# One fused attention and feed-forward kernel, its 2,679 steps put into another order

## The chip, the cores and the metric

The kernel runs on one core of one Trainium2 chip. The metric is the device time of one execution in microseconds (us), lower being better. A profiled execution also has a span, from its first to its last instruction.

## The reference

Four batches of eight heads, 768 positions, 64 values a head. Each query sees the first few keys ("sinks") and a window of up to 128 keys behind it. The result, laid out as 3072 tokens of 512 values, goes through a two-layer block with a SoLU (h times its softmax) and a layer norm between.

```python
scores = scale * np.matmul(q, k.transpose(0, 1, 3, 2))
keep = is_sink | in_window            # n_sink = 4, window = 128
a = softmax(np.where(keep, scores, -1e9)); x = np.matmul(a, v)
h = x @ w_in                          # 512 -> 1024
solu = h * softmax(h)
ln = (solu - mean(solu)) / np.sqrt(var(solu) + 1e-06) * g_ln
out = ln @ w_out                      # 1024 -> 512
```

## The kernel before, in words

The 3072 tokens are cut into 24 chunks of 128, numbered n = 0 to 23 (chunk 0 and 1 are the first chunks of two batches, then the rest follow batch by batch). A chunk goes through a long chain of steps, and the steps of some four to six chunks are under way at once:

- `turn_q`, `take_q`, `rest_q`, `swap_q`: the queries are transposed, split into a rounded high part and a rest (tile `qT`), and a copy with its halves exchanged (`qX`) is made by two DMA transfers of the SP queue.
- `take_k`, `rest_k`: the same split for the keys, into the tile `ring`.
- `score` (TensorE, 8 heads, two matmuls each, lines 656 and 657) writes into one of two PSUM banks, `bank_0` and `bank_1`. `pick` (line 663) and `mask` (line 674), both on VectorE, read the bank out; only then may another score use it.
- `exps`, `invert`, `normalise`: exponentials on ScalarE, sums inverted on VectorE, product on GpSimd. For chunks 8 to 22 that are not the first of their batch, `store_p` and `load_p` send the probabilities through DRAM (tiles `pn`, `pd`, `pb`) and `flip_p` finishes the transpose; others are transposed on TensorE (`turn_p`).
- `part_new`, `part_old` (GpSimd, lines 741 and 747) cut the transposed probabilities for two key chunks, and `value` (32 small matmuls, line 795) forms the attention output `av`.
- `x_hi`, `x_lo` (tiles `xh`, `xl`, lines 800 and 804), then `hidden` (8 steps of three matmuls, line 815), `highest`, `solu_exp`, `solu`, `centre`, `store_u`, `load_u`, `flip_u`, `u_hi`, `u_lo` (tiles `uh`, `ul`), and `project` (8 steps of three matmuls, line 902; 16 half ones in the last chunk), `scale` and `store`.

Ahead of and among the first chunks the weights are brought in: sixteen blocks are fetched (`wraw`), taken out of their 64-bit form by `lower_w` on ScalarE (line 421, tile `wps`) and `move_w`, `sign_w`, `rest_w` on VectorE (lines 425, 429, 435), and split in two parts (`w1h`, `w1l`, `w2h`, `w2l`).

What sets the order is one table. `ORDER` is a permutation of the numbers of all 2,679 steps; the kernel calls each step in turn, and each step's instructions and DMA issues go to the end of their engine's queue. Every engine works its own queue in order, so an instruction whose input isn't there holds up all that stands behind it on that engine. The pools hand out buffers in the same order.

```python
    for at in ORDER:
        f, n, i = steps[at]
        f(n, i)
```

The two score banks are handed out in the order in which they come free:

```python
    def claim(key, uses):
        held[key] = [banks.pop(0), uses]
        return held[key][0]
    def done(*key):
        held[key][1] -= 1
        if held[key][1] == 0:
            banks.append(held.pop(key)[0])
```

Of the kernel before, what the change touches and what calls it, by code (L numbers as in the profile page):

```python
# [19 lines left out]
    346, 0, 143, 2, 144, 244, 60, 348, 351, 5, 6, 3, 69, 350, 7, 51, 8, 352, 24, 9, 147, 154, 345, 12, 42, 155, 353,  # L20
    146, 156, 148, 10, 11, 61, 248, 255, 256, 257, 62, 63, 166, 15, 245, 167, 4, 182, 183, 64, 165, 160, 70, 181, 71,
    176, 66, 78, 33, 187, 72, 164, 157, 180, 158, 52, 145, 161, 186, 162, 177, 184, 163, 73, 449, 75, 178, 349, 53,
    259, 25, 54, 55, 179, 185, 26, 27, 189, 356, 87, 188, 74, 76, 77, 16, 361, 465, 28, 358, 17, 18, 191, 65, 67, 43,
    247, 360, 68, 249, 44, 45, 193, 354, 94, 19, 30, 29, 31, 57, 263, 266, 32, 136, 279, 267, 355, 34, 46, 282, 1,
    357, 359, 56, 58, 283, 268, 48, 35, 36, 453, 59, 37, 101, 79, 80, 21, 258, 47, 49, 460, 284, 81, 50, 761, 88, 82,
    190, 261, 39, 277, 262, 278, 89, 285, 90, 38, 40, 265, 264, 41, 115, 281, 280, 91, 95, 192, 194, 20, 22, 96, 362,
    97, 195, 108, 208, 286, 370, 23, 365, 246, 289, 98, 84, 291, 373, 209, 378, 381, 83, 85, 363, 210, 364, 122, 371,
    86, 293, 372, 102, 211, 379, 380, 103, 137, 138, 288, 212, 553, 213, 104, 287, 139, 116, 367, 290, 109, 215, 216,
    217, 450, 387, 375, 117, 292, 383, 110, 218, 140, 386, 461, 105, 214, 295, 294, 390, 219, 369, 462, 366, 129, 377,
    296, 374, 385, 220, 382, 118, 309, 310, 392, 402, 404, 368, 463, 221, 452, 311, 455, 454, 456, 451, 394, 396, 398,  # L30
    376, 316, 13, 317, 312, 119, 223, 92, 388, 384, 389, 347, 400, 313, 314, 458, 557, 457, 226, 93, 464, 459, 391,
    406, 554, 318, 222, 564, 111, 319, 141, 142, 130, 393, 403, 466, 395, 99, 472, 405, 474, 131, 407, 397, 555, 399,
    762, 315, 401, 224, 480, 482, 657, 408, 467, 475, 227, 488, 483, 490, 320, 470, 478, 321, 468, 409, 565, 476, 410,
    132, 486, 484, 556, 411, 471, 559, 558, 322, 412, 417, 479, 487, 492, 418, 561, 567, 473, 230, 560, 413, 123, 419,
    562, 481, 489, 493, 232, 469, 477, 566, 661, 495, 563, 414, 485, 100, 668, 415, 491, 659, 324, 124, 497, 125, 420,
    658, 494, 507, 499, 568, 576, 325, 765, 112, 865, 772, 584, 867, 126, 496, 416, 506, 508, 234, 509, 592, 501, 503,
    421, 498, 500, 572, 511, 580, 502, 504, 574, 235, 582, 588, 229, 505, 590, 422, 660, 512, 663, 423, 570, 662, 513,
    514, 578, 327, 670, 665, 667, 113, 586, 664, 666, 672, 515, 516, 228, 573, 581, 328, 425, 669, 571, 579, 133, 517,
    106, 589, 587, 594, 107, 225, 518, 519, 577, 675, 595, 671, 866, 585, 114, 521, 428, 120, 522, 523, 134, 593, 597,
    598, 868, 575, 121, 236, 237, 683, 583, 591, 596, 691, 524, 135, 676, 599, 231, 233, 600, 680, 127, 601, 426, 238,  # L40
    432, 610, 424, 429, 430, 684, 611, 692, 602, 604, 688, 612, 128, 674, 613, 520, 696, 431, 331, 682, 690, 615, 606,
    698, 764, 616, 677, 603, 605, 869, 685, 239, 525, 608, 693, 607, 333, 766, 240, 526, 241, 609, 768, 870, 242, 678,
    686, 329, 767, 330, 332, 527, 334, 617, 427, 699, 618, 769, 771, 335, 694, 702, 704, 336, 434, 770, 681, 773, 619,
    620, 679, 775, 621, 687, 433, 774, 695, 1083, 435, 776, 1092, 1091, 1094, 337, 338, 339, 436, 340, 780, 788, 700,
    341, 689, 697, 701, 706, 437, 622, 872, 1093, 703, 796, 778, 786, 871, 1189, 623, 529, 532, 781, 708, 705, 714,
    716, 794, 342, 789, 797, 873, 715, 717, 707, 803, 875, 536, 785, 709, 719, 323, 326, 779, 711, 625, 720, 787, 530,
    795, 1197, 874, 793, 624, 801, 243, 626, 784, 710, 792, 800, 627, 876, 343, 344, 878, 805, 534, 880, 783, 1199,
    782, 628, 790, 791, 713, 799, 887, 798, 1198, 884, 877, 535, 629, 883, 879, 881, 712, 1200, 630, 439, 802, 440,
    721, 885, 722, 1295, 631, 441, 723, 724, 633, 886, 806, 976, 804, 808, 818, 890, 898, 889, 977, 1082, 978, 906,
    729, 807, 725, 809, 726, 727, 980, 728, 810, 763, 634, 897, 528, 533, 905, 888, 636, 537, 1399, 730, 896, 442,  # L50
    812, 438, 820, 539, 904, 443, 932, 541, 891, 899, 1402, 907, 979, 913, 637, 981, 731, 732, 894, 982, 893, 814,
    1401, 638, 816, 819, 821, 901, 811, 813, 444, 733, 823, 815, 824, 734, 632, 445, 446, 902, 735, 447, 910, 817,
    639, 538, 825, 985, 987, 826, 909, 912, 916, 827, 543, 828, 640, 895, 540, 903, 911, 915, 918, 892, 900, 908, 448,
    1188, 829, 830, 991, 993, 1400, 914, 737, 983, 1001, 1009, 1095, 736, 833, 917, 928, 834, 919, 999, 1007, 831,
    1084, 641, 635, 929, 990, 931, 998, 542, 992, 835, 836, 1000, 1085, 1008, 921, 1006, 986, 1086, 920, 1015, 930,
    988, 923, 933, 832, 975, 934, 740, 1081, 1087, 996, 1014, 922, 1004, 531, 997, 837, 738, 1089, 925, 838, 927,
    1294, 924, 1005, 1013, 1012, 926, 1088, 1018, 544, 545, 935, 546, 547, 1017, 1020, 995, 839, 643, 994, 1403, 1002,
    1003, 1011, 1022, 936, 741, 937, 1010, 744, 548, 743, 642, 938, 549, 1016, 939, 1034, 1036, 840, 645, 1103, 1019,
    742, 841, 1100, 1511, 940, 1111, 1119, 1021, 1035, 1190, 1192, 1037, 1023, 844, 941, 942, 1099, 1194, 1025, 745,
    739, 644, 1026, 1108, 1303, 1116, 842, 550, 1305, 551, 1039, 646, 943, 1040, 1027, 944, 1107, 1115, 1304, 945,  # L60
    946, 1098, 1106, 1024, 647, 947, 1041, 1114, 1406, 746, 846, 747, 648, 1306, 1101, 1109, 1121, 1117, 649, 1122,
    650, 1029, 1028, 1030, 1032, 552, 948, 1096, 1097, 749, 748, 651, 652, 653, 1404, 654, 1104, 1112, 1105, 1113,
    1120, 1031, 1124, 1033, 1102, 1296, 1204, 1212, 1191, 655, 1042, 1043, 845, 751, 1298, 752, 1126, 847, 1128, 1140,
    1142, 848, 949, 951, 1044, 1110, 1118, 1045, 1123, 1202, 1193, 1300, 952, 1210, 1125, 1195, 1046, 1047, 843, 656,
    1220, 1205, 1218, 1048, 1127, 1129, 1213, 849, 750, 1141, 1143, 1049, 1221, 1050, 850, 950, 852, 1203, 1211, 1145,
    1208, 1146, 1051, 1297, 1052, 1216, 1224, 1219, 1053, 1209, 1227, 1217, 954, 1225, 1293, 854, 753, 754, 755, 756,
    851, 1226, 853, 1229, 1054, 1207, 1409, 1215, 1206, 1214, 1230, 1130, 1132, 855, 1232, 1133, 1131, 1223, 1222,
    1405, 1228, 757, 758, 856, 1234, 1310, 1187, 1055, 1135, 759, 1318, 1134, 1136, 1246, 1308, 957, 1138, 1299, 1301,
    1326, 857, 858, 859, 958, 1311, 1316, 1324, 955, 1057, 1147, 1058, 1248, 1231, 1137, 1309, 1417, 1408, 1139, 1410,
    1319, 1327, 1317, 1148, 956, 1325, 1332, 1412, 1233, 1235, 1510, 860, 1312, 1519, 1149, 1414, 1320, 1328, 1314,  # L70
    1322, 1419, 760, 1333, 861, 1330, 1336, 1521, 1150, 862, 1338, 1247, 1239, 1315, 1323, 1313, 1331, 1335, 1249,
    1237, 1321, 1418, 1151, 1329, 1155, 1152, 959, 1420, 960, 1411, 961, 1238, 1156, 1236, 1425, 1340, 1251, 963,
    1509, 1520, 1252, 1522, 1441, 1334, 1424, 1440, 1153, 1512, 1157, 1337, 1339, 1447, 1060, 1353, 1158, 1241, 1154,
    1243, 1341, 863, 1240, 1723, 1242, 962, 965, 966, 1355, 967, 1732, 1413, 1415, 1253, 1063, 1061, 1159, 1343, 1160,
    1244, 1245, 1254, 1344, 1617, 1625, 1523, 1345, 968, 964, 1064, 1629, 1734, 969, 1161, 1342, 864, 1255, 1162,
    1256, 1352, 1354, 1422, 1423, 1731, 1513, 1438, 1439, 1514, 1733, 970, 1428, 1444, 1446, 1429, 1445, 1257, 1515,
# [1044 lines left out]
```

## Time and profile before

| what | us |
|---|---|
| device time, median of three runs | 440.33 |
| the three runs | 438.46, 440.33, 1389.28 |
| span of the profiled execution | 437.9 |
| TensorE busy in it | 415.4 (95%) |
| VectorE busy | 360.9 (82%) |
| ScalarE busy | 315.7 (72%) |
| GpSimd busy | 234.2 (53%) |

The profile gives the span of its execution and no device time of its own beside it; the span lies 0.56 us under the fastest run and 2.43 us under the median. Busy time of TensorE is that of matmuls, whose ends are modelled and overlap; idle time is what no instruction covers. PEld stands for the weight loads of TensorE, which go beside the matmuls; a wait of a weight load that an earlier matmul outlasts costs less than it shows. DVE is VectorE, ACT ScalarE, POOL GpSimd, SPq the queue that issues the DMA transfers.

### The profile page before, as it was taken

What the parts mean: (1) busy time and instruction counts of PE and PEld (TensorE: products, weight loads), DVE (VectorE), ACT (ScalarE), POOL (GpSimd) and SP (SyncE); (2) the same over time, 40 slices, a digit from 0 to 9 for tenths busy, and PEclk for the clock granted to TensorE, in tenths of its full rate; (3) what the DMA queues carried; (4) which work ended last, traced back from release to release, by engine and by line L of the source; (5) the groups of instructions that cost most, each with busy time, mean ns of one, the idle gap of its engine ahead of it and who ended that gap; (6) DMA issues with size and microseconds to landing.
All of it is one profiled execution on the core that took longest, in us unless ns stands there. A gap on an engine that the chain in (4) does not pass through costs nothing.

```text
span 437.9 us, 8516 instructions
## 1 busy us (share of the span) xinstructions
PE 415.4 (95%) x2507; PEld 332.6 (76%) x2507; DVE 360.9 (82%) x1029; ACT 315.7 (72%) x817; POOL 234.2 (53%) x388
## 2 busy tenths in 40 slices
PE   4899999999999999999999999999999999999994
PEld 3447777878787888878777787878878778888884
DVE  2989999997999889999989997899899797674520
ACT  5989988978877776877768576768767675555551
POOL 7742626658867552788454736556623673624020
PEclk9999999999999999999999999999999999999999
DMA  8999449999899899976998989966966558623001
GB/s 225 324 284 293 96 101 168 180 151 196 218 161 216 208 185 253 195 229 190 180 239 210 207 219 226 193 173 179 269 176 216 170 165 227 188 96 121 24 26 55
DMA packets 164025, 81.38 MB, mean 186 GB/s; under 512 B 120188, under 2 KB 150788, under 8 KB 163972
## 3 DMA queue, kind: packets, MB, share of 16 engines
q1 hardware_dynamic: 163972, 80.77, 82.3%
q8 instruction: 22, 0.36, 0.4%
q14 instruction: 31, 0.25, 0.2%
HBM read 45.62 MB, written 23.72 MB: 158 GB/s over the span
## 4 chain that ended last, share of the span: by engine, by line
PE 53%; DVE 25%; DMA 6%; issue 5%; POOL 4%; ACT 4%; SPq 1%; DVEq 0%; POOLq 0%; ACTq 0%
PE o L902 18%; PE h L815 17%; PE av L795 5%; DVE qT L600 4%; DVE sc L674 3%; DVE bank L663 3%; PE bank L656 3%; PE bank L657 2%; PE ws L443 2%; DMA pb<-pd 2%; DVE ul L890 2%; DVE nm L820 2%; PE bank L654 2%; DMA wraw<-in_moe_w_in_dram 1%; DVE pt L725 1%
## 5 line engine op out<-in xcount | busy, mean ns | idle before, releaser
L685 ACT ACTIVATE sc<-sc,nmx 128x132 f32<-128x132 f32 (+1 forms) x192 | 75.9, 396 | 25.1 <-DVE nmx L674 24.1
L902 PE MATMUL o<-w2h,uh 128*128 128x512 f32 (+1 forms) x200 | 79.7, 398 | 0.0
L815 PE MATMUL h<-w1h,xh 128*128 128x512 f32 x192 | 77.0, 401 | 1.0 <-DVE u L830 0.9
L902 PE MATMUL o<-w2h,ul 128*128 128x512 f32 (+1 forms) x200 | 77.0, 385 | 0.5 <-DVE ul L890 0.5
L902 PE MATMUL o<-w2l,uh 128*128 128x512 f32 (+1 forms) x200 | 77.2, 386 | 0.0
L815 PE MATMUL h<-w1h,xl 128*128 128x512 f32 x192 | 75.9, 395 | 0.6 <-DVE xl L804 0.5
L815 PE MATMUL h<-w1l,xh 128*128 128x512 f32 x192 | 75.3, 392 | 0.0
L625 POOL TENSOR_TENSOR ring<-kf,ring 64x512 fp32r<-64x512 f32 x48 | 63.1, 1320 | 22.6 <-ACT ring L620 18.7
L674 DVE CUSTOM_DVE_ANT_0 sc<-bank,bias 128x132 f32<-128x132 f32 (+1 forms) x192 | 53.1, 288 | 9.4 <-PE bank L654 1.7
L704 POOL TENSOR_TENSOR pn<-sc,rs 128x512 f32<-128x512 f32 x26 | 28.0, 1079 | 53.1 <-DVE rs L691 19.2
L656 PE MATMUL bank<-ring,qT 128*128 128x264 f32 (+1 forms) x176 | 51.0, 300 | 1.9 <-DVE nmx L674 1.7
L657 PE MATMUL bank<-ring,qX 128*128 128x264 f32 (+1 forms) x176 | 48.3, 284 | 0.1
L700 POOL TENSOR_TENSOR sc<-sc,rs 128x528 f32<-128x528 f32 (+1 forms) x22 | 24.8, 1127 | 40.8 <-DVE rs L691 24.0
L902 PEld LDWEIGHTS o<-w2h,ul 128*128 128x128 f32 x200 | 37.5, 188 | 9.2 <-DVE ul L890 1.2
L902 PEld LDWEIGHTS o<-w2h,uh 128*128 128x128 f32 x200 | 37.6, 188 | 8.8 <-issue 3.1
L741 POOL TENSOR_SCALAR_AFFINE_SELECT pc<-pt 128x512 f32<-128x512 f32 x40 | 28.4, 716 | 29.4 <-DVE pt L725 25.5
L815 PEld LDWEIGHTS h<-w1h,xl 128*128 128x128 f32 x192 | 36.0, 188 | 10.6 <-DVE xl L804 2.8
L656 PEld LDWEIGHTS bank<-ring,qT 128*128 128x128 f32 x176 | 33.1, 188 | 12.0 <-DVE nmx L674 6.3
L815 PEld LDWEIGHTS h<-w1h,xh 128*128 128x128 f32 x192 | 36.1, 188 | 7.3 <-issue 0.8
L902 PEld LDWEIGHTS o<-w2l,uh 128*128 128x128 f32 x200 | 37.7, 188 | 5.0
L825 ACT ACTIVATE e<-h,nm 128x1024 f32<-128x1024 f32 x24 | 26.7, 1113 | 18.7 <-DVE nm L820 18.6
L815 PEld LDWEIGHTS h<-w1l,xh 128*128 128x128 f32 x192 | 36.2, 188 | 5.0
(146 smaller groups left out, 975.9 us busy)
## 6 DMA issues: line engine op xcount, KB each, us to landing
qX<-qT SPq DMA_DIRECT2D x88, 128.0 KB, 2.7
ud<-u SPq DMA_DIRECT2D x20, 512.0 KB, 4.3
ub<-ud SPq DMA_DIRECT2D x80, 128.0 KB, 3.5
pd<-pn SPq DMA_DIRECT2D x26, 256.0 KB, 3.0
pb<-pd SPq DMA_DIRECT2D x52, 128.0 KB, 3.4
vn<-in_v_dram SPq DMA_DIRECT2D x24, 256.0 KB, 4.3
out_dram<-ob SPq DMA_DIRECT2D x23, 256.0 KB, 2.6
kn<-in_k_dram SPq DMA_DIRECT2D x12, 384.0 KB, 6.6
```

The lines of the kernel that those rows point to most:

```text
L625: nc.gpsimd.tensor_tensor(t[ROWS[1 - x]], src[ROWS[x]], t[ROWS[x]].bitcast(F32), op=ALU.subtract)
L656: nc.tensor.matmul(o, st["qT", n, x][:, r, :], rhs, start=True, stop=False)
L657: nc.tensor.matmul(o, st["qX", n, x][:, r, :], rhs, start=False, stop=True)
L674: nc.vector.tensor_tensor_reduce(out=st["sc", n, hb][:, j, c0:c1], in0=st["s", n, h].rearrange("p a x -> p (a x)")[:, c0:c1], in1=bias0 if ...
L685: nc.scalar.activation(sc[:, i, c0:c1], sc[:, i, c0:c1], AF.Exp, bias=nmx[:, i:i + 1], scale=-1.0, accum_out=ssum[:, i:i + 1])
L700: nc.gpsimd.tensor_tensor(sc[:, :, c0:c1], sc[:, :, c0:c1], rs.unsqueeze(2).to_broadcast([P, HB, c1 - c0]), op=ALU.mult)
L704: nc.gpsimd.tensor_tensor(pn.rearrange("p g h f -> p h g f"), sc[:, :, 4:SEG].rearrange("p h (g f) -> p h g f", f=32), rs.unsqueeze(2).uns ...
L741: nc.gpsimd.affine_select(pc, st["pt", n, hb], pattern=[[0, HB], [1, P]], compare_op=ALU.is_ge, fill=0.0, base=0, channel_multiplier=-1)
L795: nc.tensor.matmul(acc[ROWS[x], r, :], vals[:, 2 * r + x, :], p[:, 2 * jp + x, :], start=alone, stop=alone or (r, i) == (NPAIR - 1, 1))
L815: nc.tensor.matmul(st["h", n][:, cols], a[:, kt, :], w[:, kt, cols], start=(kt == 0 and m == 0), stop=(kt == KT1 - 1 and m == 2))
L825: nc.scalar.activation(e, st["h", n], AF.Exp, bias=st["nm", n], scale=1.0, accum_out=se)
L902: nc.tensor.matmul(st["o", n, i], a[:, kt % 4, :], part(w, kt)[:, i * wide:(i + 1) * wide], start=(kt == 0 and m == 0), stop=(kt == KT2 - ...
```

## The change

The table `ORDER` is another permutation of the same 2,679 numbers; nothing else in the file differs. Each engine therefore has the same instructions, in another sequence. Two of its lines, the first before and the first after:

```diff
 ORDER = (
-    346, 0, 143, 2, 144, 244, 60, 348, 351, 5, 6, 3, 69, 350, 7, 51, 8, 352, 24, 9, 147, 154, 345, 12, 42, 155, 353,
+    143, 147, 154, 2070, 882, 1437, 3, 253, 196, 269, 1302, 2476, 203, 1431, 168, 298, 2098, 2099, 569, 301, 2102,
 )
```

In front of each name in the rows below stands the line of the code; the number in a tile's name behind the chunk (`kf_1`, `qX_16_0`) tells the chunk, the last one only the place in the program's list of tiles, which differs between the two programs.

**ScalarE at the start of the program**, before. `kf_0` and `kf_1` are the transposed keys of chunks 0 and 1 on their way out of their PSUM bank, `wps_5` is the first weight block:

```order
L615 COPY kf_0_171<-bank_1_90 128x512
L620 CAST ring_127<-kf_0_171 64x4x128 x2
L588 COPY qf_0_194<-bank_1_90 128x512
L421 ACTIVATE wps_5_211<-wraw_5_138 128x512
L615 COPY kf_1_217<-bank_0_89 128x512
L620 CAST ring_127<-kf_1_217 64x4x128 x2
```

And now:

```order
L615 COPY kf_0_135<-bank_0_89 128x512
L261 CAST ident_r_96<-ident_91 128x128
L620 CAST ring_127<-kf_0_135 64x4x128
L592 CAST qT_2_0_145<-bank_1_90 64x512
L308 COPY val_58<-spread_0_158 128x2
L592 CAST qT_2_1_188<-bank_1_90 64x512
L588 COPY qf_0_201<-bank_0_89 128x512
L310 COPY g_sb_99<-spread_1_156 128x8
L615 COPY kf_1_204<-bank_1_90 128x512
L421 ACTIVATE wps_5_206<-wraw_5_176 128x512
L620 CAST ring_127<-kf_0_135 64x4x128
```

The copy of `kf_1`, which frees the second score bank, stood behind the first weight block's lowering and now stands ahead of it.

**TensorE between the last value matmul of chunk 17 and its first hidden matmul**, before. `o_14` is the second layer's output of chunk 14, the banks take scores of chunk 19:

```order
L795 MATMUL av_17_4180<-pt_17_1_4118,vn_16_3877 64x128 x2
L902 MATMUL o_14_0_4102<-w2h_3_716,uh_14_1_4082 128x512
L902 MATMUL o_14_0_4102<-w2l_3_717,uh_14_1_4082 128x512
L902 MATMUL o_14_0_4102<-w2h_3_716,ul_14_1_4084 128x512
L656 MATMUL bank_1_90<-ring_127,qT_19_0_3951 128x264
L657 MATMUL bank_1_90<-ring_127,qX_19_0_4091 128x264
L656 MATMUL bank_0_89<-ring_127,qT_19_0_3951 128x264
L657 MATMUL bank_0_89<-ring_127,qX_19_0_4091 128x264
L815 MATMUL h_17_4241<-w1h_62,xh_17_4213 128x512
```

And now the same stretch's first rows:

```order
L795 MATMUL av_17_4129<-pt_17_1_4146,vn_16_3874 64x128 x2
L902 MATMUL o_14_0_4137<-w2h_2_745,uh_14_1_4168 128x512
L902 MATMUL o_14_0_4137<-w2l_2_746,uh_14_1_4168 128x512
L902 MATMUL o_14_0_4137<-w2h_2_745,ul_14_1_4170 128x512
L732 MATMUL ptp_18_0_4226<-ident_91,sc_18_0_3982 128x128 x4
L656 MATMUL bank_1_90<-ring_127,qT_19_0_3980 128x264
L657 MATMUL bank_1_90<-ring_127,qX_19_0_4064 128x264
L656 MATMUL bank_0_89<-ring_127,qT_19_0_3980 128x264
L657 MATMUL bank_0_89<-ring_127,qX_19_0_4064 128x264
L902 MATMUL o_14_0_4137<-w2h_2_745,uh_14_1_4168 128x512
```

One project step and two scores stood between the two; now it is four project steps (the second begins in the last row), three scores and a group of transposes.

**The SP queue at the exchange of chunk 16's queries**, before. `pn_15` is written to `pd_15` when GpSimd has normalised chunk 15; `out` is a result:

```order
L913 DMA out_0_dram<-ob_9_0_3312 128x512
L609 DMA qX_16_0_3407<-qT_16_0_3290 64x512
L610 DMA qX_16_0_3407<-qT_16_0_3290 64x512
L609 DMA qX_16_1_3425<-qT_16_1_3370 64x512
L610 DMA qX_16_1_3425<-qT_16_1_3370 64x512
L714 DMA pd_15_3449<-pn_15_0_3374 512x1x128
L862 DMA ud_12_3451<-u_12_3377 128x1024
```

And now:

```order
L714 DMA pd_15_3441<-pn_15_0_3379 512x1x128
L609 DMA qX_16_0_3443<-qT_16_0_3294 64x512
L610 DMA qX_16_0_3443<-qT_16_0_3294 64x512
L862 DMA ud_12_3460<-u_12_3317 128x1024
L536 DMA vn_15_3462<-in_v_dram 128x8x64
L714 DMA pd_15_3441<-pn_15_1_3438 512x1x128
L609 DMA qX_16_1_3558<-qT_16_1_3364 64x512
L610 DMA qX_16_1_3558<-qT_16_1_3364 64x512
```

Both exchanges of chunk 16 stood ahead of the writes of chunk 15's probabilities; each now stands directly behind one.

## Rows read from the trace of the kernel before

**Rows 1.** The page: the span, and the busy time of each engine (share of the span) with its number of instructions.

```profile
span 437.9 us, 8516 instructions
PE 415.4 (95%) x2507; PEld 332.6 (76%) x2507; DVE 360.9 (82%) x1029; ACT 315.7 (72%) x817; POOL 234.2 (53%) x388
```

**Rows 2.** Busy time by stretches of the span; behind each engine's time its number of instructions, then the granted clock, the share of the DMA engines and GB/s.

```profile
0.00:11.00 11.00, 5.38 (x21) 4.21 (x21) 2.37 (x9) 5.92 (x12) 7.72 (x31) 1.00 0.82 225
11.00:66.00 55.00, 50.69 (x270) 35.63 (x271) 52.09 (x159) 50.99 (x134) 25.51 (x34) 1.00 0.78 219
66.00:198.00 132.00, 128.65 (x824) 104.49 (x822) 120.56 (x348) 104.93 (x278) 85.94 (x128) 1.00 1.07 197
198.00:330.00 132.00, 128.96 (x782) 104.42 (x779) 119.12 (x340) 93.46 (x251) 74.40 (x122) 1.00 0.94 204
330.00:414.00 84.00, 83.44 (x509) 68.10 (x509) 61.99 (x170) 53.20 (x134) 37.99 (x67) 1.00 0.53 155
414.00:438.00 24.00, 18.31 (x108) 15.78 (x107) 4.78 (x7) 7.24 (x12) 2.70 (x8) 0.99 0.11 37
```

**Rows 3.** The waits of TensorE's weight loads from 66 to 414 us: waiting operation and line, what it waited for, us in total, times, longest.

```profile
PEld bank L656 <- DVE nmx L674: 4.8, 10, 1.2
PEld av L795 <- POOL pt L747: 3.6, 8, 0.8
...
PEld h L815 <- DVE xl L804: 2.3, 6, 0.9
...
PEld bank L657 <- DMA qX<-qT: 0.4, 1, 0.4
```

**Rows 4.** The start in order of time, TensorE, ScalarE and VectorE: start, duration, engine, line, operation, tiles, and in brackets the idle time before it with what ended it.

```profile
11.54 0.79 PE L654 MATMUL bank<-kf,qf 64*128 64x128 f32 x2 [1.50 <-ACT kf L615]
...
10.35 0.62 ACT L421 ACTIVATE wps<-wraw 128x512 f32<-128x512 f32 x1 [1.16 <-DMA wraw<-in_moe_w_in_dram]
10.91 0.58 ACT L615 COPY kf<-bank 128x512 f32<-128x512 f32 x1
...
11.01 0.70 DVE L425 TENSOR_SCALAR wps<-wps 128x512 int32<-128x512 int32 x1 [3.00 <-ACT wps L421]
12.35 0.28 DVE L674 CUSTOM_DVE_ANT_0 sc<-bank,bias 128x128 f32<-128x128 f32 x1
12.77 0.68 DVE L435 SCALAR_TENSOR_TENSOR wbits<-wraw,wps 128x512 int32<-128x512 int32 x1
```

**Rows 5.** Groups of instructions by line with shapes kept apart: count, busy us, mean ns of one, idle time before them.

```profile
L800 ACT CAST xh<-av 128x512 fp32r<-128x512 f32 x24 | 13.9, 581 | 8.6 <-PE av L795 8.4
L804 DVE TENSOR_TENSOR xl<-av,xh 128x512 fp32r<-128x512 f32 x24 | 16.3, 681 | 1.6 <-ACT xh L800 1.4
L663 DVE COPY_PREDICATED bank<-m_cur,bank 128x128 f32<-128x128 int32 x88 | 24.2, 285 | 7.7 <-PE bank L657 7.2
L674 DVE CUSTOM_DVE_ANT_0 sc<-bank,bias 128x132 f32<-128x132 f32 x160 | 44.7, 289 | 6.2 <-POOL sk L763 0.8 <-PE bank L657 0.2
L674 DVE DVE_READ_ACCUMULATOR2_ANT nmx<- 128x1 f32 x192 | 15.8, 82 | 0.0
L656 PE MATMUL bank<-ring,qT 128*128 128x264 f32 x160 | 47.2, 305 | 1.9 <-DVE nmx L674 1.7
```

**Rows 6.** Pieces of the chain of work that ended last: start, time in the chain, engine, tile, line, number of instructions.

```profile
246.39 1.90 PE av L795 x32
250.58 0.13 PE bank L656
250.71 0.12 PE bank L657
252.47 0.69 PE h L815 x3
```

**Rows 7.** What the SP queue waited for in front of its issues (us, times, longest), and the issues of the query exchange with the median us from issue to landing.

```profile
SPq L714 <- POOL sc L708: 20.3, 11, 3.7
SPq L720 <- DMA pd<-pn: 13.6, 8, 3.1
SPq L867 <- DMA ud<-u: 13.5, 6, 3.7
...
qX<-qT SPq DMA_DIRECT2D x88, 128.0 KB, 2.7
```

**Rows 8.** VectorE's two split operations with both inputs in SBUF and with one in PSUM (`bank`, `utp`), and the spread of the second over single instructions (shortest/median/longest ns).

```profile
L600 DVE TENSOR_TENSOR qT<-qf,qT 64x512 fp32r<-64x512 f32 x34 | 30.5, 898 | 2.3 <-ACT qT L592 1.3
L600 DVE TENSOR_TENSOR qT<-bank,qT 64x512 fp32r<-64x512 f32 x10 | 6.9, 689 | 2.2 <-ACT qT L592 1.9
L890 DVE TENSOR_TENSOR ul<-ur,uh 128x512 fp32r<-128x512 f32 x40 | 30.6, 772 | 3.1 <-ACT uh L886 2.9
L890 DVE TENSOR_TENSOR ul<-utp,uh 128x512 fp32r<-128x512 f32 x8 | 5.5, 686 | 10.7 <-ACT uh L886 10.6
L890 DVE TENSOR_TENSOR ul<-ur,uh x40: 651/686/1445, 101.7 to 413.6; 128x512 fp32r<-128x512 f32 x40
```

**Rows 9.** The tail: the maximum of the last chunk's hidden layer, its scaled copy on ScalarE, and the last piece of the chain.

```profile
414.49 1.23 DVE L820 TENSOR_REDUCE nm<-h 128x1 f32<-128x1024 f32 x1 [0.25 <-PE h L815]
418.31 1.15 ACT L843 ACTIVATE ud<-u,nmu 128x1024 f32<-128x1024 f32 x1 [1.30 <-DVE u L830]
...
424.57 7.75 PE o L902 x57
```

262 rows, old and new, of the table ORDER are left out of this document.

## The prediction, made before the changed kernel was run

> **What bounds the kernel now.** I read the page first: TensorE is busy 415.4 of 437.9 us [rows 1], so an order can only fight over the 22.5 us in which it has nothing to do, and over waits that hide inside its busy time. The table by stretches says where those lie [rows 2]. The first 11 us hold 5.6 us of idle TensorE. From 11 to 66 us three engines are nearly full (VectorE 52.1, ScalarE 51.0, TensorE 50.7 of 55 us): the weights are taken apart there, and VectorE has the least room. From 66 to 414 us TensorE runs 341.05 of 348 us, idle 3.35 + 3.04 + 0.56 = 6.95 us in the three rows together. The last stretch has 5.7 us of idle, nearly all after the last matmul. TensorE's granted clock is 0.99 to 1.00 in every one of these rows, that is 2.4 GHz, the idle first stretch included; I expect no term from it.
>
> The waits of TensorE's weight loads name who is late in the long middle [rows 3]: the mask that empties a score bank (4.8 us in ten waits), GpSimd's cut of the probabilities (3.6 us in eight), the rest of the attention output, `xl` (2.3 us in six). A query exchange was late once, by 0.4 us. These are the only things that another order can better there, and the first it can worsen.
>
> **The change part by part.** Every engine keeps its instructions, so no busy time goes or comes by itself. A whole table has moved, and I can't sum 2,679 moves one by one; I take the four places where rows show TensorE waiting, count in both orders how often the cause stands, and price each case from its row.
>
> *Start.* TensorE's second score waits 1.50 us for the copy of `kf_1`, since that copy (10.91 us) stands on ScalarE behind a weight block's lowering, which itself waits 1.16 us for its fetch [rows 4]. Now the copy stands ahead, so the 1.5 us go, with the 0.62 us of the lowering at most: 2.1 us for TensorE. But the stretch behind it is VectorE's. VectorE gains only what it can do in its own 3.00 us of idle time before 11.01 us: two masks, which took the 0.42 us from 12.35 to 12.77 [rows 4]. Bounds: 2.1 us gained; nothing, if the first weight block comes later than now. I take -0.4 us, the value of the engine that is full from 11 to 66 us.
>
> *Value to hidden.* The first hidden matmul of a chunk needs `xh` and `xl`, 0.58 + 0.68 = 1.26 us after the last value matmul [rows 5]. Measuring TensorE's work between them with 0.69 us for a hidden or project step and 0.25 us for a score [rows 6], 7 of the 24 chunks have less than 1.26 us before and 4 now (chunk 17 goes from one project step and two scores, 1.2 us, to 3.9 us). A case costs 2.3 us / 6 = 0.38 us [rows 3]; three fewer give -1.15 us. Bounds: 0, if what is behind `xl` is late anyway, and -2.3 us for all six.
>
> *Score banks.* A score needs the mask of the score that held its bank. I count a pair as short when TensorE's work between the two is less than VectorE's queue from that pick to that mask (0.29 us a pick, 0.29 + 0.08 us a mask, and what is put between) plus 0.30 us for the first score's own matmul [rows 5]. From chunk 3 on there are 10 short pairs before and 15 now, and what they lack adds up to 3.1 us before and 4.7 us now. I take +1.6 us. Priced by the wait's mean, 4.8 us / 10 [rows 3], the five more would be +2.4 us, the upper bound; the lower bound is 0, where VectorE runs ahead of TensorE.
>
> *The SP queue.* It waits 13.6 us for `pd` and 13.5 us for `ud` to be written before it may read them back [rows 7]. Between a chunk's last write of `pd` and the first read stand 31 other steps on SP in the 13 chunks together, 25 before; for `ud` 85 in 20 chunks, 64 before. The queue will stand still less; no large wait of TensorE names these transfers [rows 3], so I give this 0, at best -1 us. Against it, of the query exchanges that stand directly behind a write of `pd` there are 8 now and 4 before, chunk 16's two among the new ones. Such a write waits for GpSimd, 20.3 us in 11 waits [rows 7]. Directly behind a write of `ud` or a result there are 3 now and 8 before, which is why I give the whole 0. This cover, that exchanges come early, is worth the most if it is gone; that is the second rival.
>
> *Tail.* After the last hidden matmul, maximum, exponential, product and scaled copy run from 414.49 to 418.31 + 1.15 = 419.46 us, 5.0 us, and TensorE has other projects to do meanwhile; the chain ends with matmuls [rows 9]. Between that matmul and the first transpose of the last chunk there are now ten project steps, 6.9 us, where there were twelve. Still cover: 0. If it were gone, it would cost what is lacking of the 5.0 us.
>
> Sum: -0.4 - 1.15 + 1.6 + 0 + 0 = about 0, a span of 438.0 us against 437.9. The device times shown stand 0.56 and 2.43 us above the span (438.46 and the median of 440.33); with 1.5 us, midway, I forecast **439.5 us**.
>
> *A rule on shared ports.* VectorE's split takes 898 ns with both inputs in SBUF and 689 ns with one in PSUM, the other split 772 against 686 ns, and one and the same form ranges from 651 to 1445 ns [rows 8]. Something outside these instructions lengthens them, by 34 x 209 + 40 x 86 ns = 10.5 us in all. The Trainium skill, "SBUF — State Buffer", section "Who interferes with whom", says that a VectorE instruction with two SBUF inputs contends with a GpSimd instruction that reads SBUF, and that whichever comes first keeps the other out. These rows agree with it; by that rule the 10.5 us depend on which of them happen to meet, so on the order.
>
> **The rivals.** *Faster by over 2%.* All 6.95 us of idle between 66 and 414 us go, and 2.1 us at the start with them: 439.5 - 9.05 = 430.5 us. For it speaks that the DMA read-backs have more room; against it that this takes nearly every wait of the middle, while the count of short bank pairs goes up, and that the first 66 us belong to VectorE, not to TensorE.
>
> *Slower by over 2%: the query exchange comes late.* An exchange needs 2.7 us from issue to landing and now stands four times more behind a write that waits for GpSimd, a mean of 20.3 / 11 = 1.85 us and at most 3.7 us [rows 7]. If each such wait reaches TensorE, it costs 7.4 to 14.8 us; taking the middle, 439.5 + 11 = 450.5 us. It decides once the wait exceeds the lead that the exchange has over its first score. Against it: that wait was 0.4 us in the whole middle [rows 3], and fewer exchanges now stand behind results.
>
> *More meetings on the ports.* If twice as many of the two-input splits are lengthened, VectorE has 10.5 us more to do [rows 8]. It is idle 11.4 us of 132 in the first of the middle's stretches and more later [rows 2], so about half would reach TensorE: 439.5 + 5.3 = 444.8 us, 1% slower. The opposite, all lengthening gone, gives 434.3 us.
>
> *The change does less than the table suggests.* Both orders keep each chunk's steps within a few us of the same place in TensorE's work, and the waits just land elsewhere; that is my forecast in other words, and gives the same time.
>
> **How the numbers follow.** Two per cent of 440.33 is 8.8 us, about what a measurement of this kernel can tell from no change. The forecast, within 2% with waits that move but add up to the same, gets 0.72; ports that meet more or less often 0.05, also within 2%. The faster rival gets 0.10: it needs every gain at once. The slower one gets 0.13: a new order of this size has more ways to lose a lead than to find one in an engine that is 95% busy, but its counts are mixed. So faster 0.10, same 0.77, slower 0.13. The range of 432 to 450 us covers the forecast, both port cases (434.3 and 444.8) and the slower rival up to its middle, and leaves out the faster one and the rest of the slower one, about 0.16.
>
> **What would show it.** In the changed profile: TensorE busy close to 415 us, and 5 to 9 us idle between 66 and 414 us; the 1.50 us wait for `kf_1` gone, with VectorE's first weight step still near 11 us; weight loads waiting for `xl` under 2.3 us and for the bank's mask over 4.8 us; the tail's last piece again one run of matmuls. I am wrong if a weight load waits for `qX` by several us (the exchange), if VectorE's busy time leaves 361 us by over 5 us (the ports), or if a long wait stands in the tail.

## The result, and the profile after

The changed kernel takes 428.29 us (median of four runs, 427.67 to 429.0), the kernel before 441.46 us beside it (438.46 to 1389.28, four runs); the ratio is 0.9735, with a 95% interval of 0.9692 to 0.9778. It is 2.65% faster, below the range that I gave. The run of 1389.28 us stands far off all the others and is left out of the ratio. The profiled execution took 428.25 us, 1.75 us more than its span.

The page of the changed kernel: span and busy times, to be read against [rows 1].

```profile
span 426.5 us, 8500 instructions
PE 410.2 (96%) x2507; PEld 333.3 (78%) x2507; DVE 347.4 (81%) x1029; ACT 313.4 (73%) x817; POOL 231.9 (54%) x388
```

The span is 11.4 us shorter. VectorE does the same 1,029 instructions in 13.5 us less, and TensorE's busy time fell by 5.2 us, which, with equal instructions at an equal clock, speaks for waits that had been hidden inside it (the ends of matmuls are modelled).

The same stretches as in [rows 2], changed kernel.

```profile
0.00:11.00 11.00, 5.45 (x21) 4.00 (x21) 2.36 (x9) 4.91 (x11) 7.25 (x30) 1.00 0.84 214
11.00:66.00 55.00, 51.23 (x273) 35.94 (x272) 50.43 (x156) 52.15 (x135) 25.04 (x35) 1.00 0.81 226
66.00:198.00 132.00, 131.47 (x852) 109.11 (x852) 120.12 (x364) 108.58 (x289) 88.55 (x134) 1.00 1.05 202
198.00:330.00 132.00, 132.00 (x815) 109.64 (x815) 119.15 (x357) 96.80 (x265) 76.39 (x126) 1.00 0.96 220
330.00:414.00 84.00, 83.17 (x503) 68.19 (x500) 54.31 (x145) 49.36 (x119) 33.89 (x63) 1.00 0.42 123
```

From 66 to 330 us TensorE is idle 0.53 us, where it was idle 6.39 us, and it gets 1,667 matmuls done there instead of 1,606. The start hardly differs.

The chain of work that ended last, by engine, before and then after: TensorE's own work now makes up 81% of it, and VectorE's share fell from a quarter to a twentieth.

```profile
PE 53%; DVE 25%; DMA 6%; issue 5%; POOL 4%; ACT 4%; SPq 1%; DVEq 0%; POOLq 0%; ACTq 0%
```

```profile
PE 81%; ACT 6%; DVE 5%; issue 3%; DMA 2%; POOL 1%; SPq 1%; DVEq 0%; ACTq 0%; POOLq 0%
```

The waits of TensorE's weight loads from 66 to 414 us, changed kernel, against [rows 3]: all three that I had named fell, the one for the mask most.

```profile
PEld bank L656 <- DVE nmx L674: 1.6, 6, 0.5
...
PEld av L795 <- POOL pt L747: 1.4, 5, 0.4
...
PEld h L815 <- DVE xl L804: 0.6, 2, 0.4
```

VectorE's operations that come out shorter, changed kernel, against [rows 8]; the last line adds a constant to four numbers a row (`rs`), and its row of before stands behind it.

```profile
L600 DVE TENSOR_TENSOR qT<-qf,qT 64x512 fp32r<-64x512 f32 x34 | 26.0, 765 | 1.2
...
L890 DVE TENSOR_TENSOR ul<-ur,uh 128x512 fp32r<-128x512 f32 x40 | 28.8, 729 | 2.5 <-ACT uh L886 2.5
...
L690 DVE TENSOR_SCALAR rs<-ssum 128x4 f32<-128x4 f32 x48 | 8.9, 185 | 1.2 <-ACT sc L685 1.0
```

```profile
L690 DVE TENSOR_SCALAR rs<-ssum 128x4 f32<-128x4 f32 x48 | 11.8, 246 | 2.8 <-ACT sc L685 2.8
```

The means fell from 898 to 765, from 772 to 729 and from 246 to 185 ns, with the same instructions on the same shapes. I call *lengthening* what single VectorE instructions take above the median of their line, where that is over 60 ns. Summed over the trace it is 17.6 us in 38 instructions before and 6.0 us in 21 after; of the 17.6 us, 11.0 stand beside one GpSimd instruction, the subtraction of the keys' low part (line 625), of the 6.0 us 2.6. One such meeting in the trace of before, GpSimd, VectorE and a weight load in order of time:

```profile
200.50 4.68 POOL L625 TENSOR_TENSOR ring<-kf,ring 64x512 fp32r<-64x512 f32 x3
200.56 1.78 DVE L600 TENSOR_TENSOR qT<-qf,qT 64x512 fp32r<-64x512 f32 x1
202.37 0.29 DVE L674 CUSTOM_DVE_ANT_0 sc<-bank,bias 128x128 f32<-128x128 f32 x1
...
202.72 0.19 PEld L656 LDWEIGHTS bank<-ring,qT 128*128 128x128 f32 x1 [0.38 <-DVE nmx L674]
```

GpSimd starts 0.06 us ahead; VectorE's split takes 1.78 us instead of 0.69; the mask behind it in VectorE's queue is late; and the weight load of the next score stands 0.38 us. Counted over the single instructions of the trace of before, all 38 lengthened ones run beside a GpSimd instruction that had begun no later. Of VectorE's 74 splits with two SBUF inputs (lines 600 and 890), 14 begin inside a subtraction of line 625, and 13 of these are lengthened; in the changed order 6 begin so, and 5 are. GpSimd is lengthened in its turn, counted in the same way by 17.2 us before and 15.4 us now, 12.8 and 12.0 us of it beside those two splits. So the engines still meet; what got rarer is that VectorE is the one that waits. This is the chain that the experiments had to confirm or break.

### The profile page after: what moved, and what is told of

Read it like the earlier page. It is cut to its first block, busy times and chain, and to the rows that moved or that the text cites. A ratio compares the mean times of both kernels' runs of the same rounds, so it can differ in the third digit from the quotient of the medians.

```text
span 426.5 us, 8500 instructions
## 1 busy us (share of the span) xinstructions
PE 410.2 (96%) x2507; PEld 333.3 (78%) x2507; DVE 347.4 (81%) x1029; ACT 313.4 (73%) x817; POOL 231.9 (54%) x388
## 4 chain that ended last, share of the span: by engine, by line
PE 81%; ACT 6%; DVE 5%; issue 3%; DMA 2%; POOL 1%; SPq 1%; DVEq 0%; ACTq 0%; POOLq 0%
PE o L902 29%; PE h L815 26%; PE av L795 9%; PE bank L656 5%; PE bank L657 4%; PE ptp L732 2%; ACT sc L685 1%; PE bank L561 1%; PE bank L654 1%; PE av L784 1%; PE ws L443 1%; ACT ring L620 1%; DMA ud<-u 1%; DMA kn<-in_k_dram 1%; DMA ub<-ud 1%
## 5 line engine op out<-in xcount | busy, mean ns | idle before, releaser
L902 PE MATMUL o<-w2h,uh 128*128 128x512 f32 (+1 forms) x200 | 78.8, 394 | 0.0
L704 POOL TENSOR_TENSOR pn<-sc,rs 128x512 f32<-128x512 f32 x26 | 28.9, 1112 | 44.7 <-ACT sc L685 10.9
L741 POOL TENSOR_SCALAR_AFFINE_SELECT pc<-pt 128x512 f32<-128x512 f32 x40 | 25.7, 651 | 27.2 <-DVE pt L725 20.1
```

Source lines behind the costliest of these rows:

```text
L704: nc.gpsimd.tensor_tensor(pn.rearrange("p g h f -> p h g f"), sc[:, :, 4:SEG].rearrange("p h (g f) -> p h g f", f=32), rs.unsqueeze(2).uns ...
L741: nc.gpsimd.affine_select(pc, st["pt", n, hb], pattern=[[0, HB], [1, P]], compare_op=ALU.is_ge, fill=0.0, base=0, channel_multiplier=-1)
L902: nc.tensor.matmul(st["o", n, i], a[:, kt % 4, :], part(w, kt)[:, i * wide:(i + 1) * wide], start=(kt == 0 and m == 0), stop=(kt == KT2 - ...
```

## The experiments

Two theories about the 11.4 us of the span. **P (ports):** the new order makes fewer of VectorE's instructions meet GpSimd's reads, VectorE gets shorter, and TensorE's waits go with that. **L (leads):** the new order gives the hand-offs more distance, meetings or not. Before that, where in the program the gain lies: **M**, behind 66 us, against **S**, a better start. All ratios are to the kernel before, run in the same batch (in the batches of the experiments its medians lay between 438.81 and 440.8 us).

| kernel | lengthening, us | of it beside line 625 or what replaces it | median, us | ratio, 95% interval |
|---|---|---|---|---|
| before | 17.6 | 11.0 | | 1 |
| changed | 6.0 | 2.6 | 428.29 | 0.9735, 0.9692 to 0.9778 |
| s_ab | 15.2 | 10.0 | 440.01 | 1.001, 0.9986 to 1.0033 |
| s_ba | 8.0 | 3.5 | 429.89 | 0.9771, 0.9718 to 0.9825 |
| s_mid | 12.6 | 7.5 | 435.22 | 0.9893, 0.985 to 0.9936 |
| b_ms | 8.7 | 0.7 | 432.3 | 0.9816, 0.9763 to 0.987 |
| b_ms3 | 8.3 | 2.3 | 433.93 | 0.9863, 0.9821 to 0.9905 |
| b_q | 11.5 | 6.7 | 435.71 | 0.9885, 0.9865 to 0.9904 |
| b_qk | 5.8 | 0.4 | 431.62 | 0.9783, 0.9764 to 0.9802 |
| a_ms | 3.8 | 0.7 | 429.47 | 0.9752, 0.9702 to 0.9803 |
| a_q | 3.4 | 0.7 | 428.25 | 0.9725, 0.9704 to 0.9746 |
| a_more | 6.1 | 3.3 | 439.88 | 0.9979, 0.9963 to 0.9995 |
| a_sub2 | 21.8 | 16.9 | 466.96 | 1.0584, 1.0525 to 1.0644 |
| a_sub_ms | 13.0 | 10.0 | 470.65 | 1.0704, 1.0652 to 1.0755 |
| b_restk | 17.8 | 9.6 | 450.0 | 1.025, 1.0211 to 1.0289 |
| a_restk | 9.5 | 6.1 | 450.59 | 1.0265, 1.0231 to 1.0298 |
| b_pool_ms | 7.9 | 0.8 | 455.33 | 1.0374, 1.0341 to 1.0407 |
| a_pool_ms | 5.6 | 0.5 | 445.93 | 1.0163, 1.0127 to 1.02 |

**Where the gain lies.** Three tables joined from the two orders. 2,557 of the 2,679 steps issue something; the others go to the end.

```diff
-ORDER = (order before)
+ORDER = (first 400 working steps of before, then the rest as in the changed order)   # s_ba
+ORDER = (first 400 working steps of the changed order, then the rest as before)      # s_ab
+ORDER = (first 1,275 working steps of before, then the rest as in the changed order) # s_mid
```

s_ba: 

> The first 400 working steps in the order before (to about 68 us), the rest in the changed order. Theory M (the gain lies behind 66 us, where TensorE's hidden and open stalls fell from 13.2 to 3.2 us): 428 to 431 us. Theory S (a better start sets up the rest): 437 to 441 us.

s_ab: 

> The first 400 working steps in the changed order (to about 68 us), the rest in the order before. Theory M: 437 to 441 us, no gain. Theory S: 428 to 431 us.

s_mid: 

> The first 1,275 working steps in the order before (to about 205 us), the rest in the changed order. If the gain is spread over the middle like VectorE's lengthening (8.3 us in 66 to 198, 7.8 us in 198 to 330 us before; 3.1 and 2.6 after), half of it: 433 to 436 us. If it comes from one place, 429 or 439 us.

Measured 429.89, 440.01 and 435.22 us. The new start alone is worth nothing, the new rest most of it (M; 2.29% of 2.65%), and a switch at about 205 us somewhat under half of it. The joined table of s_mid shows the gain arise stretch by stretch; its two rows of the middle are like [rows 2] up to the switch (TensorE 128.34 us) and near the changed kernel behind it:

```profile
66.00:198.00 132.00, 128.34 (x824) 104.44 (x823) 120.51 (x346) 104.69 (x279) 85.27 (x129) 1.00 1.03 197
198.00:330.00 132.00, 131.04 (x801) 108.32 (x800) 117.98 (x352) 98.65 (x264) 75.90 (x122) 1.00 0.96 216
```

**The meetings taken away, GpSimd's side.** The subtraction of line 625 becomes memsets of the same region, in the order before (b_ms, b_ms3 with a third line) and in the changed one (a_ms). The keys' low part is left out.

```diff
-        nc.gpsimd.tensor_tensor(t[ROWS[1 - x]], src[ROWS[x]], t[ROWS[x]].bitcast(F32), op=ALU.subtract)
+        nc.gpsimd.memset(t[ROWS[1 - x]].bitcast(F32), 0.0)
+        nc.gpsimd.memset(t[ROWS[1 - x]].bitcast(F32), 0.0)
```

b_ms: 

> The order before, with GpSimd's subtraction of the keys' low part (line 625, 48 times, two SBUF inputs, about 1.29 us) replaced by two memsets of the same region, which read no SBUF; the keys' low part is left out, and the other instructions stay. Theory P (ports: VectorE's two-input splits and small ops are lengthened where they meet this GpSimd instruction, 11.0 of 17.6 us in the trace of before, and TensorE's waits in the middle follow from that): VectorE's busy time falls from 361 us to about 350 and the time to 430 to 434 us. Theory L (leads: the new order gives each hand-off more distance, meetings or not): the lengthening goes, but the time stays at 438 to 442 us, since the order that makes TensorE wait is still there.

a_ms: 

> The changed order with the same replacement of line 625 by two memsets. Control: only 2.6 us of VectorE's lengthening stand beside line 625 there. Theory P: 426 to 428 us, within 1 us of the changed kernel, VectorE busy about 345 us. Theory L: 427 to 429 us, no difference from the changed kernel.

b_ms3: 

> The order before, with line 625 replaced by three memsets of its region, by the run with two about 0.52 us each, so 1.56 us against the 1.29 us of the subtraction: GpSimd has more to do than before and still reads no SBUF there; the keys' low part is left out. Theory P (ports): 430 to 434 us, as with two memsets (432.3). Theory G (the run with two was faster because GpSimd had 17 us less to do and handed over earlier): the gain goes, 437 to 442 us.

Measured 432.3, 429.47 and 433.93 us. The old order gains 7 us without a step moved, the changed one nothing (1.2 us above its median, past both theories' marks): P, and not L alone. With three memsets GpSimd is busy 241.0 us, more than before, and most of the gain stays, so that it wasn't the shorter busy time of GpSimd (theory G). The 1.6 us between b_ms3 and b_ms come from two batches, and the intervals of their ratios overlap: a price of that time is not shown. VectorE is busy 353.1 us in b_ms, where about 350 was expected, and 345.0 us in a_ms.

One thing these memsets change besides: they read nothing, so they wait for no input. GpSimd stood 18.7 us in front of line 625 for ScalarE's half of the keys (`ring`, line 620) before, and in b_ms it stands 5.2 us in front of the first memset. That this earlier GpSimd made the gain is unlikely, since TensorE's wait for its `pt` did not fall (3.6 us [rows 3], now 3.7 us), while the wait for VectorE's mask fell from 4.8 to 2.8 us. In b_ms, 66 to 414 us:

```profile
PEld av L804 <- POOL pt L756: 3.7, 8, 1.1
...
PEld bank L665 <- DVE nmx L683: 2.8, 7, 0.7
```

The replacement on VectorE's side, next, leaves GpSimd's subtraction and its waits in place; VectorE's own idle time in front of those splits was 2.3 us [rows 8].

**The meetings taken away, VectorE's side.** The split of line 600 with two SBUF inputs becomes two memsets of about its length, with GpSimd's work untouched (b_q, and a_q in the changed order); b_qk has both replacements. Low parts are left out. a_more keeps the changed order whole and adds those memsets in front of 18 splits.

```diff
+        if not turned(n):                      # b_q, a_q, b_qk: in place of the split
+            nc.vector.memset(t[ROWS[1 - x]].bitcast(F32), 0.0)
+            nc.vector.memset(t[ROWS[1 - x], 0].bitcast(F32), 0.0)
+        if not turned(n) and n % 2:            # a_more: the two memsets ahead of the split
```

b_q: 

> The order before, with VectorE's split of the transposed queries (line 600, the 34 with two SBUF inputs) replaced by two memsets of the same length together (about 0.66 us, an estimate from the memsets at the program's start, against 0.69 us); the queries' low part is left out for these chunks, GpSimd's work is untouched. Theory P (ports): 7.2 of the 17.6 us of lengthening go, and what the lock costs GpSimd with them: 431 to 435 us. Theory L (the order, not the meetings): 438 to 441 us.

a_q: 

> Control: the changed order with the same replacement at line 600; 2.6 us of lengthening stand there. Theory P: 426.5 to 428.5 us. Theory L: 427.5 to 429 us.

b_qk: 

> The order before with both replacements, line 600 and line 625 by memsets (the low parts of keys and queries are left out). Theory P alone: lengthening under 6 us and 427 to 430 us, all of the gain without any change of order. Ports and order together: 431 to 433 us, as with line 625 alone, and waits of weight loads for GpSimd's `pt` stay at 3 us or more where the changed order has 1.4 us.

a_more: 

> The changed order with two additional memsets on VectorE (about 0.66 us together, no SBUF input) ahead of 18 of the splits of line 600, one in each half of chunks 7, 9, ... 23: 11.9 us more for VectorE, spread over 105 to 355 us, without a meeting. If VectorE's time in the middle is worth one to one there, as a line through the runs so far has it: 437 to 440 us. If the changed order has room for it on VectorE (its waits for TensorE's bank rose from 11.0 to 14.9 us): 428.5 to 432 us, and then less lengthening was worth so much before only because that order had no such room.

Measured 435.71, 428.25, 431.62 and 439.88 us. b_q missed its expected interval by 0.7 us on the upper side and lies on the side of P; with both replacements the order before comes to 431.62 us. That is 9.2 of the 12.5 us between the two orders in this batch (440.8 us, and a_q, which stands for the changed order, 428.25 us), with as little lengthening of VectorE as the changed order has. The lengthening of GpSimd falls there too, to 8.6 us (15.4 us in the changed order), so that the 9.2 us are the worth of the meetings on both engines, not of VectorE's side alone. The 3.4 us that are left are no meetings: ports and order together, as the expectation put it, though its mark of 3 us for `pt` was not met. The waits of weight loads in b_qk, 66 to 414 us:

```profile
PEld bank L661 <- DVE nmx L679: 2.7, 9, 0.5
PEld av L800 <- POOL pt L752: 2.6, 7, 0.8
...
PEld ptp L737 <- POOL sc L705: 1.0, 2, 0.7
```

So of the wait for the mask, 4.8 us before [rows 3], 2.1 us went with the meetings; the changed order without these meetings, a_q, has 1.0 us. Of the 3.6 us for `pt`, 1.0 us went with them, and 1.2 us more in the changed order.

a_more tells what VectorE's time is worth in the changed order. The memsets it adds take 8.7 + 3.0 us, the lengthening stays at 6.1 us, and the kernel takes 11.6 us longer:

```profile
L601 DVE MEMSET qT<- 64x512 f32 x18 | 8.7, 485 | 2.0 <-issue 1.0 <-DMA out_dram<-ob 0.2 <-DMA ud<-u 0.2
...
L602 DVE MEMSET qT<- 64x128 f32 x18 | 3.0, 165 | 1.5
```

```profile
PEld bank L659 <- DVE nmx L677: 6.6, 10, 1.1
```

One to one, and the wait that comes back is that for the mask. In a_q, on the other hand, VectorE is busy 341.7 us, 5.7 us less than in the changed kernel, and nothing is gained; TensorE works 132.00 of 132 us there too:

```profile
198.00:330.00 132.00, 132.00 (x822) 109.86 (x822) 116.62 (x372) 96.56 (x266) 73.92 (x126) 1.00 0.95 218
```

The changed order stands at the point where VectorE hardly holds TensorE up any more; what VectorE gets beyond it costs in full. In the order before the price is lower: the 9.2 us of b_qk came with 11.8 us less lengthening of VectorE, about 0.8 to one.

**Experiments that told nothing apart.** Two tried to bring meetings back into the changed order by doubling the subtraction, with added memsets as control:

```diff
         nc.gpsimd.tensor_tensor(t[ROWS[1 - x]], src[ROWS[x]], t[ROWS[x]].bitcast(F32), op=ALU.subtract)
+        nc.gpsimd.tensor_tensor(t[ROWS[1 - x]], src[ROWS[x]], t[ROWS[x]].bitcast(F32), op=ALU.subtract)   # a_sub2
+        # a_sub_ms: three memsets of the region ahead of one subtraction
```

a_sub2: 

> The changed order, with the subtraction of line 625 issued twice (the same instruction, the same result): 48 x 1.29 = 62 us more of GpSimd with two SBUF inputs, in the same places. Theory P: meetings with VectorE's splits come back, VectorE's busy time rises from 347 us to 352 or more, and the time to 432 to 440 us. Theory L: only what a later hand-off of the keys costs, within 1 us of the next run.

a_sub_ms: 

> The changed order, with three memsets of the same region (about 1.56 us) ahead of each subtraction of line 625, control for the run with the subtraction twice: GpSimd has 75 us more to do and no more meetings. Theory P: VectorE busy 346 to 349 us, 428 to 431 us, at least 2 us below the doubled subtraction. Theory L: as much as or more than the doubled subtraction, since the keys come later still.

Measured 466.96 and 470.65 us. No theory had a number near these for either. The doubled subtraction has more lengthening than its control, as P says, and VectorE is busy 363.4 us in it; but the control has more too (13.0 us, and VectorE 354.5 us instead of 346 to 349), and what sets both times, 39 and 42 us above the changed kernel, is GpSimd's own time: the key transposes of VectorE wait for the tile `kf` to be read, and TensorE for the keys. The wait in a_sub2, and the same wait in the changed kernel (66 to 414 us):

```profile
DVE kf L566 <- POOL ring L626: 16.9, 7, 3.9
```

```profile
DVE kf L566 <- POOL ring L625: 1.2, 2, 0.9
```

An engine that is busy 54% of the span had no room for 62 us more in these places. A part of the loss goes with TensorE's clock: its granted clock is 0.97 and 0.96 of its upper level, 2.4 GHz, in the two stretches of the middle of a_sub2, where TensorE is idle for 8.44 and 12.45 us, and at 1.00 in the changed kernel:

```profile
66.00:198.00 132.00, 123.56 (x763) 99.81 (x763) 109.24 (x332) 95.88 (x261) 95.76 (x130) 0.97 0.95 177
198.00:330.00 132.00, 119.55 (x698) 97.17 (x698) 112.02 (x304) 87.68 (x231) 100.74 (x137) 0.96 0.86 192
```

The other four moved one engine's steps alone from one order into the other, as far as data and buffers allow; in two of them all of GpSimd's steps, with line 625 as memsets (the keys' low part is left out there).

```diff
-ORDER = (order before)
+ORDER = (order before, its 48 rest_k steps at their places of the changed order)              # b_restk
+ORDER = (order before, all of GpSimd's steps towards their places of the changed order)       # b_pool_ms
+ORDER = (changed order, its 48 rest_k steps at their places of before)                        # a_restk
+ORDER = (changed order, all of GpSimd's steps towards their places of before)                 # a_pool_ms
```

b_restk: 

> The order before with only the 48 key subtractions (`rest_k`, line 625) moved: each stands between the same numbers of other steps as in the changed order, as far as its data allow. Theory P (ports): the time follows VectorE's lengthening one to one, as it did so far (6.0 us and 428.3; 8.0 and 429.9; 12.6 and 435.2; 15.2 and 440.0; 17.6 and 440): where these places are what avoids the meetings, the lengthening falls to 8 to 12 us and the time to 430 to 435. Theory R (the meetings hang on all engines' orders together, not on the subtraction's place): lengthening 14 to 20 us, 437 to 442 us. A time that falls without the lengthening, or the other way, speaks against P.

a_restk: 

> The changed order with only the 48 key subtractions moved to the places that they have in the order before. Theory P with the place as cause: lengthening 12 to 18 us, 434 to 440 us. Theory R: lengthening 5 to 9 us, 428 to 432 us.

b_pool_ms: 

> The order before with all of GpSimd's steps moved towards their places in the changed order (130 of 271 neighbours are then those of the changed order, 62 those of before), and line 625 as two memsets (the keys' low part left out). Theory Q (the 4 us that the memsets left over against the changed order, 432.3 to 428.3, are GpSimd's hand-offs: weight loads waited 3.7 us for `pt` there and 1.4 us in the changed order): 428 to 430.5 us, waits for `pt`, `pc` and `sc` under 4 us together. Without Q: 432 to 434 us.

a_pool_ms: 

> The changed order with GpSimd's steps moved towards their places in the order before (174 of 271 neighbours are then those of before, 66 those of the changed order), and line 625 as two memsets (the keys' low part left out). Theory Q: 432 to 434 us, waits for `pt`, `pc` and `sc` 5 us or more together. Without Q: 428.5 to 430 us, as the changed order with memsets.

Measured 450.0, 450.59, 455.33 and 445.93 us: all slower than both kernels, outside every expectation, with a lengthening of 17.8, 9.5, 7.9 and 5.6 us, which does not order these times. What stands out in them are long waits for GpSimd's tiles at the foreign places; that these are what makes them slow is read from the waits, and no run tested it. A wait of b_restk, one of b_pool_ms and one of a_pool_ms (66 to 430 us):

```profile
PEld bank L656 <- POOL ring L625: 4.9, 4, 2.0
```

```profile
PEld av L796 <- POOL pt L748: 14.9, 12, 4.8
```

```profile
PEld av L796 <- POOL pt L748: 7.1, 9, 3.0
```

The place of the subtractions alone is thus not what avoids the meetings (b_restk has 17.8 us of lengthening), and in these four runs an order could not be taken over one engine at a time.

## Why the prediction was wrong, by its steps

**Bound.** The 6.95 us of idle TensorE time between 66 and 414 us were read rightly, but taken as the most that an order could win there. Adding up what lies between one TensorE step's start and the next, above what such a step usually takes, gives some 10 us less from 66 to 414 us in the changed kernel than before. The sums themselves hang on what is taken as usual (the expectation of s_ba has 13.2 and 3.2 us; other measures give larger sums), their difference hardly does. Of the 10 us, 5.6 are idle time (6.95 us before, 1.36 us now); the rest lay inside busy time. I had named hidden waits and put no number to them.

**Start, -0.4 us.** Right in size: s_ab has the new start and gains nothing. The wait for `kf_1` is 0.29 us instead of 1.50 us, but VectorE's first weight step starts at 12.12 us instead of 11.01 us [rows 4], which I had named as the end of the bounds at nothing. The other bound, 2.1 us, was too wide: a wait of 1.50 us can give back no more than itself.

**Value to hidden, -1.15 us.** Right in sign, and inside its bounds: the wait for `xl` went from 2.3 us [rows 3] to 0.6 us. The count of chunks was not the whole cause, since with VectorE's meetings down to the changed order's the order before has 1.0 us (b_qk, three waits).

**Score banks, +1.6 us.** Wrong in sign: the wait for the mask fell from 4.8 to 1.6 us, and I had set a rise above 4.8 us as the mark. The step that failed is VectorE's queue counted in fixed durations, 0.29 us a pick and 0.37 us a mask. The mask was late, often, because a VectorE instruction ahead of it took longer: in the 5 us before six of the ten waits, 3.7 of the 4.8 us, one ended that was lengthened by 0.5 to 1.1 us; a pair that is short by the count is filled if VectorE runs ahead, which I had as the lower bound.

**SP queue, 0.** Right: no weight load of the middle waits for a query exchange in the changed kernel; the slower rival, 450.5 us, did not come about. **Tail, 0.** Close: from the last maximum to the end there are 22.6 us, 23.4 before.

**Ports.** This was the cause, and the step that failed is its price and its chance. The prediction had the 10.5 us of lengthening [rows 8] and a rule that explains them, and then let only half reach TensorE, because VectorE is idle 11.4 us of 132 [rows 2]. That idle time was no room: VectorE waits in it for TensorE's next score (11.0 us in 14 waits from 66 to 414 us before), while TensorE waits for VectorE's masks. In the trace of before:

```profile
DVE bank L663 <- PE bank L657: 11.0, 14, 2.0
```

The measured price is 11.6 us for 11.7 us in the changed order (a_more) and about 0.8 to one in the order before (b_qk), not one half. "All lengthening gone", 434.3 us by the prediction, would have been 429 us at full price and 431 us at 0.8; the lengthening fell by 11.6 us, and with ports alone the order before reaches 431.62 us. And a chance of 0.05 for both directions took VectorE's loss in the meetings for something that a new order leaves about as it is. It fell to a third.

**The rivals.** "Faster", 430.5 us, came nearest in time. Its middle was right, the idle time of the middle did go; the 2.1 us at the start, which it needed for its sum, did not, and the time lost inside TensorE's busy time was not in it. That its number lies 2.2 us from the result is in part luck.

What stays open: which hand-offs carry the 3.4 us between b_qk and the changed order, beyond the waits shown, and what in the new order lets VectorE lose fewer of its meetings; moving the subtractions alone did not do it.

## What to carry to other kernels

Before counting steps, compare the mean of each operation with its median and longest: where equal instructions take different times, something outside them is at work, and its sum belongs in the forecast at nearly full price (0.8 to 1.0 here) if the engine is in a closed loop with the one that sets the end, that is, if each of the two waits for the other in turn. Idle time of such an engine isn't room, as long as the wait in it is for the other engine of the loop. And judge an order over all engines together: one engine's steps in another order's places came out worse than both orders, while tables joined at one point in time (s_ba, s_mid) lay between them.

## What the runs showed of the hardware

A VectorE instruction as small as 128 x 4 with one SBUF input (line 690) is lengthened too, from a median of 166 ns to 1169 ns at most in the trace of before, beside line 625; the prediction had counted two-input splits alone. The Trainium skill, "SBUF — State Buffer", section "Who interferes with whom", lists `tensor_scalar` among the operations that can take the port pair shared with GpSimd, and the trace agrees. VectorE's transpose of 128 x 512 with one input (line 566) stayed between 668 and 712 ns in 34 instances, though 26 of them ran beside a GpSimd instruction, and the ten splits of line 600 with one input in PSUM between 684 and 694 ns. GpSimd's memsets of 64 x 512, which read nothing, took 0.52 us each. Of the two-input splits 18 began inside one in b_ms and b_ms3, and one of these was lengthened, which ran on beside two further GpSimd instructions. The small `rs` was lengthened by memsets too: the 0.7 us beside them in b_ms and the 2.3 us in b_ms3 are all its own, three and seven instances of 324 to 561 ns, each ending within 0.05 us of its memset.

```profile
L690 DVE TENSOR_SCALAR rs<-ssum x48: 126/166/1169, 20.1 to 398.9; 128x4 f32<-128x4 f32 x48
```
